# Second MLP stage of the last two token tiles: seven block products in place of eight, result feature-major, whole work order recomputed

## The chip, the cores and the metric

One NeuronCore of one Trainium2 chip runs the whole program. The metric is the device time of one execution in microseconds (us), lower is better. Engines: PE is TensorE (matmuls; PEld is its weight load), DVE is VectorE, ACT is ScalarE, POOL is GpSimd, SP issues most of the DMAs.

## What is computed

Inputs are q, k, v of shape (8 batches, 8 heads, 576 tokens, 64) and three weights, all float32. First comes linear attention with random features, then an MLP with SiLU on the 8 x 576 = 4608 tokens of width 512:

```
phi(x) = exp(h - max(h)) / sqrt(m),  h = x @ omega.T - |x|^2 / 2
num = phi(q) @ (phi(k).T @ v);  den = phi(q) @ sum(phi(k)) + 1e-6
x = num / den            # (4608, 512)
h = x @ w_in             # (4608, 2048)
g = h * sigmoid(h)
out = g @ w_out          # (4608, 512)
```

## The kernel before, in words

**Attention.** Two heads of a batch make a window; there are 32 (NWIN), four to a batch. Window n of batch t gives a quarter of the inner dimension of token tile t. The denominators of a window are ten small DVE operations (L437).

**Precision.** A float32 operand a is kept as two parts, a high one (rounded to fp32r) and a low one (the rest). A product of two such operands is three matmuls: high x high, low x high, high x low. Every MLP matmul below streams 512 columns.

**MLP, plain.** Nine token tiles of 512 tokens: tile t holds the first 512 tokens of batch t, tile 8 the last 64 of every batch. A step (t, f) belongs to token tile t and one 128-wide block f of the 2048 hidden features (16 blocks). The first stage of a step is 12 matmuls (four inner quarters x three, L633), then ACT makes SiLU twice (L743 as the rounded high part, L746 or L748 in full) and an elementwise subtraction gives the low part (L754), then the second stage is 12 matmuls (four groups of 128 tokens x three, L762) into four PSUM banks "acc". Tiles 0 to 2 (PLAIN = 3) run in this way. While tile 0 runs, the weights are loaded, converted on DVE (L595 to L601) and split on POOL (L614, L618); the parts of w_out go to DRAM (`keep_weight`) and are fetched again, 512 KB for each step (`get_weight`, L625, ring "wo" of four).

**MLP, pairs.** Tiles (3,4), (5,6) and (7,8) are taken in pairs p = 0, 1, 2. Their first stage is a two-by-two block product with seven in place of eight block multiplications (Strassen's way, in Winograd's form): the blocks are the two token tiles, two neighbouring feature blocks f = 2s and 2s + 1, and two halves of the inner dimension. For each of the eight s, `product` (L694 to L707) makes seven products of six matmuls each (L704), some added up in the same PSUM bank; ACT copies the first (`first_copy`, L711), DVE does five sums (`gather`, L730). The combined weights are prepared on POOL and ACT and kept in DRAM (`spread`, `spread_split`; L648 to L675), and come back as 28 transfers of 512 KB (`get_stream`, L692, rings x00 to x30). The combined token blocks are made at the start of a pair (`combine`, L555; `operand_high`, L562; `operand_low`, L566). The second stage of a pair is plain: 2 tiles x 16 steps x 12 matmuls. Half of it (the first tile of the pair) stands between the seven products of its s, the other half follows.

**The order.** All instructions are units of a planner (`Plan`). A unit has an engine, an estimated duration, a due time (its key), what it waits for, and the ring buffers and PSUM banks it takes. `run` goes through a model of the chip and takes at each point, among the units that could start earliest on their engine, the one with the lowest key. What it returns is the fixed instruction order of every engine, the DMA queue of SP among them. The keys come from constants (SLOW, STRETCH, PACE and others, L65 to L86) and from `shift_keys`, which moves some keys by random amounts from a list of seeds (SHIFTS). Which PSUM banks (there are eight: acc 4, att 2, h 1, fx 1) a unit may take is in `banks_of` (L97).

**The end.** The last four output banks (tile 8) are copied half by ACT (L775), half by DVE (L776), one after the other, and sent on two queues (L779).

Of the kernel before, what the change touches and what calls it, by code (L numbers as in the profile page):

```python
# [9 lines left out]
F32 = mybir.dt.float32  # L10
F32R = mybir.dt.float32r
# [8 lines left out]
P = 128  # L20
# [31 lines left out]
for _f in range(16):  # L52
# [6 lines left out]
)  # L59
EARLY_HOMES = ("wre", "wre", "hx", "s1")  # L60
STREAM = ((0, 0), (4, 1), (1, 0), (5, 1), (3, 2), (6, 1), (2, 2))
START_MLP = 54.5
SLOW = 8.26
MLP_STEP = 2.725
PRO = 11.00  # L65
SWITCH = 1.3
STAY = 7.1
# [3 lines left out]
    23, 57, 87, 139, 192, 248, 273, 481, 555, 701, 731, 750, 770, 866, 909, 936, 1096, 1151, 1552, 1831, 1917,  # L71
    1932, 2134, 2341, 2437, 2587, 2640, 270948, 271140, 273159, 273591,
# [5 lines left out]
def clock(step):  # L78
    return START_MLP + SLOW * step


STRETCH = (1.309, 1.051, 0.945)
# [3 lines left out]
PACE = ((0, clock(0)), (4, 185.0), (16, clock(NF * PLAIN) - 7.8), (24, BEGIN[1] - 8.8), (28, BEGIN[2] - 11.7))  # L86
# [22 lines left out]


def product_time(p, s, i):
    at = (0.0, 1.5, 3.3, 5.2, 8.0, 10.0, 12.5)[i]
    return BEGIN[p] + STRETCH[p] * (5.5 * MLP_STEP * s + at)


def second_time(i, j=0):
# [5 lines left out]
    if p == PAIRS:  # L122
        return BEGIN[-1]
# [15 lines left out]
class Plan:  # L139
# [16 lines left out]
    def run(self, until=None, heat=None):  # L156
# [46 lines left out]
        while any(ready.values()):  # L203
# [81 lines left out]
def attention_mlp(ctx: ExitStack, tc: tile.TileContext, qT, kT, qn, kn, v, om_in, w_in, w_out, out):  # L285
# [340 lines left out]

    def stage1(t, f, k, *ps):
# [61 lines left out]

    def get_stream(p, q):  # L690
        T["ws", p, q] = ws = new(f"x{(28 * p + q) % 4}0", [P, 2, 2, 2 * P], F32R)
        nc.sync.dma_start(ws.bitcast(F32), ws_d[q].bitcast(F32))  # L692
# [62 lines left out]

    def stage2(t, f, j):
        if f == 0 and (t or not j):
            T["po", t] = T.get(("po", t), []) + [bank("acc") for _ in range(1 if t else 4)]
        js = slice(j * P, (j + 1) * P)
        gh, gl, wo = T["gh", t, f], T["gl", t, f], T["wo", t, f]  # L760
        for n, (g, w) in enumerate(((gh, wo[:, 0]), (gh, wo[:, 1]), (gl, wo[:, 0]))):
            nc.tensor.matmul(  # L762
                T["po", t][j], g[:, js], w, start=f == 0 and n == 0, stop=f == NF - 1 and n == 2
            )

    def store(t, j):
        po = T["po", t][j]
        if t < B:
            ot = new("ot", [P, DMODEL])
            T["ot", t, j] = ot  # L770
            nc.scalar.copy(ot, po)
            return
        ot = ring.tile([P, DMODEL], F32, tag=("hk", "hq")[j % 2], name="ot", bufs=2)
        h = DMODEL // 2
        nc.scalar.copy(ot[:, :h], po[:, :h])  # L775
        nc.vector.tensor_copy(ot[:, h:], po[:, h:])  # L776
        for i in range(2):
            r = (2 * j + i) * S + MAIN
            (nc.sync, nc.scalar)[i].dma_start(out[r : r + REST], ot[i * REST : (i + 1) * REST])  # L779
# [20 lines left out]
    for n in range(NWIN):  # L800
# [95 lines left out]
        add(("den", n), "DVE", 2.9, at(n, 8, 34.2), lambda n=n: denom(n), after=e["q"] + [zn],  # L896
# [42 lines left out]
    def weight(i, key, src, last, more=()):  # L939
# [12 lines left out]
        add(("wh",) + i, "POOL", 0.64, key - 1, lambda: weight_high(i), after=[("wd",) + i + (2,)], alloc=list(more))  # L952
        add(("wlo",) + i, "POOL", 1.29, key, lambda: weight_low(i), after=[("wh",) + i], free=[("w32",) + i])

    last = None
    for f in range(NF):
        key = clock(f)
        weight(("in", f), key - 4, w_in[f], last)
# [9 lines left out]
    def products(p, s):  # L968
        for i, (c, b) in enumerate(STREAM):
            q, half = divmod(7 * s + i, 2)  # L970
            if half == 0 or i == 0 and s == 0:
# [4 lines left out]
                    after=sources, order=order, alloc=[(f"x{(28 * p + q) % 4}0", ("ws", p, q))], lat=2.1)  # L976
# [5 lines left out]
            if half or (i == 6 and s == NS - 1):  # L982
                free = free + [("ws", p, q)]
            add(m, "PE", 1.365, product_time(p, s, i), lambda *ps, p=p, s=s, i=i: product(p, s, i, *ps), after=after,
                order=order, banks=1 if i in (0, 1, 4) else 0, of="h", free=free)
            due = product_time(p, s, i) + 1.5
            if i == 0:
                add(("c1", p, s), "ACT", 0.62, due, lambda p=p, s=s: first_copy(p, s), after=[m], alloc=[("s1", ("s1", p, s))])
            else:
                for what, x in (("U2", 1), ("U3", 3), ("C22", 4), ("C21", 5), ("C12", 6)):  # L990
# [4 lines left out]
                    if what == "U2":  # L995
                        alloc = [(tags[0], ("u", p, s))] if len(tags) == 1 else [(tags[j], ("u", p, s, j)) for j in range(2)]
                    extra = {"U2": [("c1", p, s)], "C22": [("U3", p, s)], "C12": [("U2", p, s)], "C21": [("U3", p, s)]}.get(what, [("U2", p, s)])
                    free = {"C21": [bk(("m", p, s, 1))], "C12": [bk(("m", p, s, 4))]}.get(what, [])
                    add((what, p, s), "DVE", 0.69, due, lambda p=p, s=s, w=what: gather(p, s, w), after=[m] + extra, alloc=alloc, free=free)
# [3 lines left out]

    sums_of = ("odd", "S1", "even", "S2", ("split", 0), ("split", 1), "S3", ("split", 2), "even2", "S4", ("split", 3))
    for s in range(NS):
        before = ("sp", s - 1, len(sums_of) - 1) if s else ("wlo", "out", NF - 1)
        base = clock(NF + 2 + 3.3 * s)
# [33 lines left out]
    for p in range(PAIRS):  # L1041
# [8 lines left out]
        for q in range(2):  # L1050
# [19 lines left out]
            for i, (kind, what, after) in enumerate(work):  # L1070
# [9 lines left out]
                else:  # L1080
                    on = "POOL" if i % 4 == 1 else "DVE"
# [9 lines left out]
    for i, (t, f) in enumerate(steps):  # L1091
        key = clock(i)
        late = i >= total - LAG
# [32 lines left out]
        for j in range(4):  # L1126
            k2 = second_time(i, j)
            if late:
                k2 = BEGIN[-1] + 4 + 4 * j + i - total
# [8 lines left out]
            if f == NF - 1:  # L1138
                add(("store", t, j), "ACT", 0.62, k2 + 0.2, lambda t=t, j=j: store(t, j), after=[("s2", t, f, j)],
                    alloc=[("ot", ("ot", t, j))] if t < B else [], free=[("po", t, j)])  # L1140
                if t < B:
                    add(("send", t, j), "SP", 0.36, k2 + 1, lambda t=t, j=j: send(t, j), after=[("store", t, j)], lat=1.1,
                        free=[("ot", t, j)])
# [9 lines left out]
_OUT = ((B * S, DMODEL), "float32")  # L1153

# [47 lines left out]
```

## Time and profile before

| | before |
|---|---|
| median of 3 runs | 1064.47 us (1063.26 to 1065.71) |
| the profiled execution | 1064.04 us, of which span 1062.3 us |
| mean granted TensorE clock | 0.986 |
| PE busy | 96% of the span |
| DVE, ACT, POOL busy | 61%, 55%, 39% |
| first matmul of a block product (L704) | 477.5 us |
| first block product of the last pair | 885.6 us |

The span runs from the first instruction to the last; 1.7 us of the time lie around it. A busy share is an average over stages. The records of matmuls overlap (each is modelled with its latency), so 96% does not say that PE runs at its best rate; the distance between the starts of matmuls does.

### The profile page before, as it was taken

The page shows a single profiled execution, that of the slowest core. Times are in us where ns is not written, and L with a number is a line of the kernel's source. Part 1 is how long each engine was busy: PE and PEld are TensorE (multiplying, and loading weights), DVE is VectorE, ACT ScalarE, POOL GpSimd, SP SyncE. Part 2 cuts the span into 40 slices and gives each one's busy share as a digit, 9 for nine tenths or more (in the row PEclk, how much of TensorE's full clock was granted, in tenths as well). Part 3 has the DMA queues.
Part 4 walks back from the last instruction along what each step waited for, and adds up shares of the span by engine and source line. Part 5 has one row for each costly group of instructions (what it writes and reads, how often), then busy time and mean ns, then how long its engine had stood idle before and what let it go on. Part 6 is the DMA issues. An engine that isn't in the chain of part 4 may idle for free.

```text
span 1062.3 us, 16989 instructions
## 1 busy us (share of the span) xinstructions
PE 1024.3 (96%) x5926; PEld 820.4 (77%) x5926; DVE 643.9 (61%) x1665; ACT 587.1 (55%) x1033; POOL 418.7 (39%) x467
## 2 busy tenths in 40 slices
PE   6889899999999999999999999999999999999998
PEld 6667777777777777777878777788888878888886
DVE  6898798967767678777676676764535233232200
ACT  4777676656666666666545567754244464221253
POOL 2443564556565665333223245641211453000042
PEclk9788999999999999999999999999999999999999
DMA  8567565575765766557666667566554566755374
GB/s 290 186 222 234 171 213 180 194 254 181 243 222 189 240 195 210 165 180 269 205 202 196 203 204 258 176 216 215 170 174 160 193 214 207 230 187 198 116 237 139
DMA packets 82277, 216.14 MB, mean 203 GB/s; under 512 B 12944, under 2 KB 19216, under 8 KB 82192
## 3 DMA queue, kind: packets, MB, share of 16 engines
q1 hardware_dynamic: 81728, 214.47, 61.5%
q8 instruction: 47, 0.77, 0.3%
q10 hardware_dynamic: 464, 0.59, 0.2%
q14 instruction: 38, 0.31, 0.1%
HBM read 181.47 MB, written 33.55 MB: 202 GB/s over the span
## 4 chain that ended last, share of the span: by engine, by line
PE 84%; DVE 9%; issue 2%; ACT 2%; DMA 1%; POOL 1%; ACTq 0%; DVEq 0%; SPq 0%; POOLq 0%
PE ps_acc L762 33%; PE ps_h L704 11%; PE ps_fx L704 11%; PE ps_h L633 8%; PE ps_att L355 5%; DVE prod L437 4%; PE ps_att L449 3%; PE ps_att L511 2%; PE ps_att L473 2%; PE ps_fx L633 1%; PE ps_fx L473 1%; PE ps_att L362 1%; PE ps_att L420 1%; DVE nbk L376 1%; DVE mxk L371 1%
## 5 line engine op out<-in xcount | busy, mean ns | idle before, releaser
L762 PE MATMUL ps_acc<-wo,gh 128*128 128x512 f32 x1152 | 365.3, 398 | 0.0
L762 PEld LDWEIGHTS ps_acc<-wo,gh 128*128 128x128 f32 x1152 | 209.0, 188 | 43.5
L762 PE MATMUL ps_acc<-wo,gl 128*128 128x512 f32 x576 | 225.2, 391 | 0.0
L704 PE MATMUL ps_h<-w,x 128*128 128x512 f32 x504 | 130.3, 394 | 0.0
L704 PE MATMUL ps_fx<-w,x 128*128 128x512 f32 x504 | 130.1, 393 | 0.0
L633 PE MATMUL ps_h<-x,w 128*128 128x512 f32 x492 | 128.3, 402 | 0.0
L762 PEld LDWEIGHTS ps_acc<-wo,gl 128*128 128x128 f32 x576 | 108.1, 188 | 23.4
L467 POOL TENSOR_TENSOR hq<-hq,rd 128x384 f32<-128x384 f32 x96 | 83.1, 893 | 107.0 <-DVE rd L442 61.7
L704 PEld LDWEIGHTS ps_fx<-w,x 128*128 128x128 f32 x504 | 93.4, 188 | 19.9
L704 PEld LDWEIGHTS ps_h<-w,x 128*128 128x128 f32 x504 | 93.2, 188 | 20.1
L633 PEld LDWEIGHTS ps_h<-x,w 128*128 128x128 f32 x492 | 91.3, 191 | 20.2 <-ACT gf L746 0.2
L754 POOL TENSOR_TENSOR gl<-s,gh 128x512 fp32r<-128x512 f32 x24 | 31.0, 1290 | 191.0 <-ACT s L748 127.9
L754 DVE TENSOR_TENSOR gl<-gf,gh 128x512 fp32r<-128x512 f32 x72 | 57.6, 801 | 35.6 <-ACT gf L746 34.6
L437 DVE CUSTOM_DVE_ANT_0 prod<-hq,ps_att 128x128 f32<-128x128 f32 (+1 forms) x190 | 54.5, 287 | 33.0 <-ACT kw L462 13.8
L411 POOL TENSOR_TENSOR t<-hk 128x256 f32<-128x256 f32 x48 | 35.3, 757 | 98.4 <-ACT hk L405 98.4
L743 ACT ACT_TABLE_LOAD x49 | 62.9, 1283 | 1.4 <-PE ps_acc L762 0.6
L485 ACT COPY en<-ps_att 128x384 f32<-128x384 f32 x61 | 28.7, 486 | 56.9 <-PE ps_att L473 52.3
L743 ACT ACTIVATE gh<-ps_h 128x512 fp32r<-128x512 f32 x53 | 31.7, 598 | 48.2 <-PE ps_h L704 32.1
L743 ACT ACTIVATE gh<-s 128x512 fp32r<-128x512 f32 x24 | 15.2, 632 | 77.2 <-DVE s L730 70.3
L405 ACT ACT_TABLE_LOAD x40 | 51.3, 1283 | 2.0 <-DVE hk L396 1.3
L343 ACT ACTIVATE nat<-nat 128x576 f32<-128x576 f32 x64 | 42.8, 693 | 14.6 <-DMA nat<-kn 8.0
L675 POOL TENSOR_TENSOR wraw<-w,wraw 128x256 fp32r<-128x256 f32 x32 | 25.0, 782 | 53.3 <-ACT wraw L673 47.8
(245 smaller groups left out, 1820.4 us busy)
## 6 DMA issues: line engine op xcount, KB each, us to landing
wo<-wo_d SPq DMA_DIRECT2D x128, 512.0 KB, 3.9
x<-ws SPq DMA_DIRECT2D x84, 512.0 KB, 3.5
rawq<-qT SPq DMA_DIRECT2D x32, 352.0 KB, 4.0
rawk<-kT SPq DMA_DIRECT2D x32, 352.0 KB, 3.4
v<-v SPq DMA_DIRECT2D x32, 320.0 KB, 3.8
nat<-kn SPq DMA_DIRECT2D x32, 288.0 KB, 3.9
nat<-qn SPq DMA_DIRECT2D x32, 288.0 KB, 4.1
wraw<-w_in SPq DMA_DIRECT2D x16, 512.0 KB, 3.6
```

Source lines behind the costliest of these rows:

```text
L343: nc.scalar.activation(nat, nat, AF.Square, scale=SCALE * 0.5**0.5)
L355: nc.tensor.matmul(ps[:, i * M : (i + 1) * M], raw[r, o : o + P], oms[r], start=True, stop=True)
L405: nc.scalar.activation(h, h, AF.Exp)
L411: nc.gpsimd.tensor_tensor(t[:, j], e[:, 5 * j : 5 * j + 2], e[:, 5 * j + 2 : 5 * j + 4], ALU.add)
L437: nc.vector.tensor_tensor_reduce(out=prod[r], in0=e[r, c], in1=z[r, j * M : (j + 1) * M], scale=1.0, scalar=GUARD, op0=ALU.mult, op1=ALU.a ...
L467: nc.gpsimd.tensor_tensor(e[:, c], e[:, c], rd[:, c].unsqueeze(2).broadcast_to([P, 3, M]), ALU.mult)
L473: nc.tensor.transpose(ps[:, off + i * P : off + (i + 1) * P], T["h", n, "q"][:, 3 * g + i], ident)
L633: nc.tensor.matmul(ph, w[:, i], x[:, j], start=k == 0 and n == 0, stop=k == NK - 1 and n == 2)
L704: nc.tensor.matmul(ph, ws[:, u, kk * P : (kk + 1) * P], o[:, x], start=i in (0, 1, 4) and kk == 0 and n == 0, stop=kk == 1 and n == 2, ski ...
L743: nc.scalar.activation(gh, ph, AF.Silu)
L754: eng.tensor_tensor(gl, block(t, f) if held is None else held, T["gh", t, f].bitcast(F32), ALU.subtract)
L762: nc.tensor.matmul(T["po", t][j], g[:, js], w, start=f == 0 and n == 0, stop=f == NF - 1 and n == 2)
```

## The change

- The last pair's second stage becomes a block product too. Blocks: the two token tiles, two halves of 256 output features, and odd and even hidden blocks f; the eight s are added up in PSUM. Seven products i, each over s = 0 to 7, six matmuls for each (i, s) (`second`): 56 groups of six. The weight is now the stationary operand and the tokens are streamed, so that the result has features on partitions; it goes to an output of its own, `out_t`, which the host turns and puts in its place.
- The first stage of that pair now runs whole before the second (a matmul of product (0, 0) of the second stage is ordered behind the last product of the first); it may take any of the eight PSUM banks. ACT makes SiLU once in place (`whole_silu`, four for each s). DVE makes four sums for each s (`g_sum`: T3, T1, T2, T4). Then for each of the 56 groups ACT makes the high part (`g_high`) and DVE the low part (`g_rest`), in rings of three buffers.
- Combined blocks of w_out are made in the same way: the plain w_out is kept in DRAM while it is first converted (`keep_plain`, 16 transfers of 256 KB; a w32 buffer is now also held until that transfer is done), fetched later (`get_plain`, 16), combined on POOL (`spread_out`, 32 operations; `split_out`, 32 on POOL and 32 on ACT) and kept (`keep_out`, 32 transfers of 256 KB). `get_second` brings 28 x 512 KB: one transfer for products 1, 3, 4, 6, two of 256 KB for products 0, 2, 5. The 32 transfers of `get_weight` for tiles 7 and 8 are gone.
- The end: the last two result blocks are each added by DVE from PSUM (`q_out`) and sent in two parts.
- All planner constants and the list of seeds are new; some estimated durations and the model of DMA time are changed. So the order on every engine is new from the start.

The diff, cut to its core:

```diff
-START_MLP = 54.5
-SLOW = 8.26
+START_MLP = 54.500
+SLOW = 8.020
 MLP_STEP = 2.725
-PRO = 11.00
+PRO = 11.770
 SWITCH = 1.3
-STAY = 7.1
+STAY = 10.900
...
-PACE = ((0, clock(0)), (4, 185.0), (16, clock(NF * PLAIN) - 7.8), (24, BEGIN[1] - 8.8), (28, BEGIN[2] - 11.7))
+PACE = ((0, clock(0)), (4, PAIRS_4), (16, clock(NF * PLAIN) - PAIRS_16), (24, BEGIN[1] - PAIRS_24), (28, BEGIN[2] - PAIRS_28))
...
+    if u["of"] == "full":
+        return ["h", "fx", "att", "acc"]
...
-                pipe = max(pipe, t + dur + 1.0) + u["lat"]
-                done = max(pipe, t + dur + 2.2)
+                pipe = max(pipe, t + dur + 1.0) + 0.75 * u["lat"]
+                done = max(pipe + 0.25 * u["lat"], t + dur + 2.2)
...
+    def keep_plain(f):
+        nc.sync.dma_start(plain_d[f], T["w", ("out", f)])
+
+    def get_plain(s, odd):
+        T["plain", s, odd] = w = new(("gf", "w32")[odd], [P, 2, 2 * P])
+        nc.sync.dma_start(w.rearrange("p a b -> p (a b)"), plain_d[2 * s + odd])
...
+    def spread_out(s, what):
+        a11, a12, a21, a22 = plain_blocks(s)
+        if what == "S1":
+            T["S12o", s] = new("s1", [P, 2, 2 * P])
+        s1, s2 = (T["S12o", s][:, j] for j in range(2))
+        out, x, y = {"S1": (s1, a21, a22), "S2": (s2, s1, a11), "S3": (a11, a11, a21), "S4": (a12, a12, s2)}[what]
+        nc.gpsimd.tensor_tensor(out, x, y, ALU.add if what == "S1" else ALU.subtract)
+    def split_out(s, i, high):
+        if high:
+            T["spo", s, i] = new("ot", [P, 2, 2 * P], F32R)
+        g = T["spo", s, i]
+        a11, a12, _, _ = plain_blocks(s)
+        a = (T["S12o", s][:, 0], T["S12o", s][:, 1], a11, a12)[i]
+        if high:
+            nc.scalar.copy(g[:, 0], a)
+        else:
+            nc.gpsimd.tensor_tensor(g[:, 1], a, g[:, 0].bitcast(F32), ALU.subtract)
+
+    def keep_out(s, i):
+        nc.sync.dma_start(ws2_d[4 * i + s // 2][:, s % 2].bitcast(F32), T["spo", s, i].bitcast(F32))
...
+    def get_second(p, q):
+        T["wt", p, q] = ws = new(f"x{q % 4}0", [P, 2, 2, 2 * P], F32R)
+        i, s2 = divmod(q, NS // 2)
+        if i in (1, 3, 4, 6):
+            nc.sync.dma_start(ws.bitcast(F32), ws2_d[4 * {4: 0, 1: 1, 3: 2, 6: 3}[i] + s2].bitcast(F32))
+            return
+        odd, j = {0: (0, 0), 2: (1, 0), 5: (1, 1)}[i]
+        for x in range(2):
+            f = 4 * s2 + 2 * x + odd
+            nc.sync.dma_start(ws[:, x].bitcast(F32), wo_d[f][:, :, 2 * P * j : 2 * P * (j + 1)].bitcast(F32))
...
+    def whole_silu(p, s, i):
+        u = T["u", p, s]
+        src, dst = (
+            (T["pb", p, s, 0], T["b", p, s][0]), (T["s1", p, s], T["b", p, s][1]), (u[0], u[0]), (u[1], u[1]),
+        )[i]
+        nc.scalar.activation(dst, src, AF.Silu)
...
+        out, a, b, op = {
+            "T3": (x, b22, b12, ALU.subtract), "T1": (b12, b12, b11, ALU.subtract), "T2": (b11, x, b11, ALU.add),
+            "T4": (b21, b21, b11, ALU.subtract),
+        }[what]
+        nc.vector.tensor_tensor(out, a, b, op)
...
+        return (b11, b11, b21, T.get(("t3", p, s)), b12, b21, b22)[i]
+
+    def g_high(p, i, s):
+        T["qh", p, i, s] = h = new("gh", [P, MAIN], F32R)
+        nc.scalar.copy(h, g_block(p, i, s))
+
+    def g_rest(p, i, s, eng):
+        T["ql", p, i, s] = l = new("gl", [P, MAIN], F32R)
+        eng.tensor_tensor(l, g_block(p, i, s), T["qh", p, i, s].bitcast(F32), ALU.subtract)
+
+    def second(p, i, s, *ps):
+        chain = (0, 1, 0, 1, 2, 1, 2)[i]
+        if ps:
+            T["qb", p, chain] = ps
+        w = T["wt", p, i * NS // 2 + s // 2][:, s % 2]
+        h, l = T["qh", p, i, s], T["ql", p, i, s]
+        for d in range(2):
+            for n, (u, x) in enumerate(((0, h), (0, l), (1, h))):
+                nc.tensor.matmul(
+                    T["qb", p, chain][d], w[:, u, d * P : (d + 1) * P], x, start=i in (0, 1, 4) and s == 0 and n == 0,
+                    stop=s == NS - 1 and n == 2, skip_group_check=True,
+                )
...
+        ps = T["qb", p, {"C11": 0, "C21": 1, "C22": 2, "C12": 2}[what]][d]
+        T["ot", p, what, d] = ot = new("ot", [P, MAIN])
+        if what == "C11":
+            nc.scalar.copy(ot, ps)
+        else:
+            other = {"C21": T.get(("q1", p, d)), "C22": T.get(("U3", p, d)), "C12": T.get(("U2", p, d))}[what]
+            nc.vector.tensor_tensor(ot, ps, other, ALU.add)
...
-            add(("sums", n), "POOL", 3.3, at(n, 6, 25), lambda n=n: sums(n), after=e["k"], order=[("sums", n - 1)] if n > DIRECT else [],
+            add(("sums", n), "POOL", 3.4, at(n, 6, 25), lambda n=n: sums(n), after=e["k"], order=[("sums", n - 1)] if n > DIRECT else [],
...
-        add(("den", n), "DVE", 2.9, at(n, 8, 34.2), lambda n=n: denom(n), after=e["q"] + [zn],
+        add(("den", n), "DVE", 3.5, at(n, 8, 34.2), lambda n=n: denom(n), after=e["q"] + [zn],
...
+        if i[0] == "out":
+            add(("k32", i[1]), "SP", 0.36, key, lambda: keep_plain(i[1]), after=[("wd",) + i + (2,)], lat=1.1, free=[("w32",) + i])
...
-                order=order, banks=1 if i in (0, 1, 4) else 0, of="h", free=free)
+                order=order, banks=1 if i in (0, 1, 4) else 0, of="full" if full else "h", free=free)
...
+            ready = (W(0), G("T2"), W(1), G("T3"), G("T1"), G("T4"), W(3))
+            for i in range(7):
+                add(H(i), "ACT", 0.62, t1(i, s) - (4 if i else 10), lambda p=p, i=i, s=s: g_high(p, i, s), after=[ready[i]],
+                    order=[("qh", p, i, s - 1)] if s else [("qh", p, i - 1, NS - 1)] if i else [],
+                    alloc=[("gh", ("qh", p, i, s))])
+                on = "DVE"
+                add(L(i), on, 1.3 if on == "POOL" else 0.66, t1(i, s) - (3 if i else 9),
+                    lambda p=p, i=i, s=s, e=on: g_rest(p, i, s, nc.gpsimd if e == "POOL" else nc.vector),
+                    after=[H(i)], order=[("ql", p, i, s - 1)] if s else [("ql", p, i - 1, NS - 1)] if i else [],
+                    alloc=[("gl", ("ql", p, i, s))], port=True)
...
+                after = [("gt", p, q), ("qh", p, i, s), ("ql", p, i, s)]
+                if s == 0:
+                    after += {
+                        2: [("q1", p, d) for d in range(2)], 3: [("qU2", p, d) for d in range(2)],
+                        5: [("qU3", p, d) for d in range(2)], 6: [("qC22", p, d) for d in range(2)],
+                    }.get(i, [])
+                add(("m2", p, i, s), "PE", 1.365, t1(i, s), lambda *ps, p=p, i=i, s=s: second(p, i, s, *ps), after=after,
+                    order=[("m2", p, i, s - 1)] if s else [("m2", p, i - 1, NS - 1)] if i else [("m", p, NS - 1, 6)],
+                    banks=2 if i in (0, 1, 4) and s == 0 else 0, of="full",
+                    free=[("qh", p, i, s), ("ql", p, i, s)] + ([("wt", p, q)] if half else []))
...
+    out_steps = ("S1", "S2", ("split", 0), ("split", 1), "S3", ("split", 2), "S4", ("split", 3))
+    for s in range(NS):
+        base = BEGIN[PAIRS - 1] + SPREAD_AT + SPREAD_OUT * s
...
-                    on = "POOL" if i % 4 == 1 else "DVE"
+                    on = "POOL" if i % 4 == 1 and p < PAIRS - 1 else "DVE"
...
-    steps = [(t, f) for t in range(B + 1) for f in range(NF)]
+    steps = [(t, f) for t in range(PLAIN + 2 * PAIRS - 2) for f in range(NF)]
...
+    for s in range(NS):
+        products(PAIRS - 1, s)
+    second_stage(PAIRS - 1)
```

## Rows read from the trace of the kernel before

**Rows 1.** The page: busy time, and the clock in 40 slices.
```profile
PE 1024.3 (96%) x5926; PEld 820.4 (77%) x5926; DVE 643.9 (61%) x1665; ACT 587.1 (55%) x1033; POOL 418.7 (39%) x467
...
PEclk9788999999999999999999999999999999999999
```

**Rows 2.** Busy us (count) of PE, PEld, DVE, ACT, POOL, then clock, DMA, GB/s.
```profile
0.00:120.00 120.00, 100.76 (x715) 80.10 (x715) 97.26 (x273) 73.78 (x196) 47.95 (x57) 0.87 0.67 222
120.00:480.00 360.00, 347.24 (x2187) 272.87 (x2189) 272.63 (x732) 234.72 (x400) 193.45 (x235) 1.00 0.63 206
480.00:880.00 400.00, 399.17 (x2248) 321.03 (x2247) 234.51 (x605) 223.24 (x344) 140.63 (x147) 1.00 0.62 203
880.00:1057.00 177.00, 177.00 (x782) 146.38 (x780) 39.05 (x57) 55.01 (x93) 36.70 (x29) 1.00 0.57 187
```

**Rows 3.** The chain of waits, 1000 to 1063 us: start, us, what.
```profile
1005.44 47.61 PE ps_acc L762 x210
...
1057.37 0.38 ACT ot L775
...
1057.77 0.42 DVE ot L776
```

**Rows 4.** Groups by shape, 890 to 1057 us: count, busy us, mean ns.
```profile
L762 PE MATMUL ps_acc<-wo,gh 128*128 128x512 f32 x272 | 83.7, 389 | 0.0
...
L704 PE MATMUL ps_fx<-w,x 128*128 128x512 f32 x168 | 42.6, 389 | 0.0
...
L754 DVE TENSOR_TENSOR gl<-gf,gh 128x512 fp32r<-128x512 f32 x8 | 5.5, 692 | 17.8 <-ACT gf L746 17.8
...
L748 ACT ACTIVATE s<-s 128x512 f32<-128x512 f32 x8 | 5.1, 632 | 0.3
...
L730 DVE TENSOR_TENSOR w<-ps_fx,w 128x512 f32<-128x512 f32 x4 | 2.8, 692 | 7.4 <-PE ps_fx L704 7.4
...
L711 ACT COPY s<-ps_fx 128x512 f32<-128x512 f32 x4 | 2.4, 588 | 6.3 <-PE ps_fx L704 3.4 <-POOL gl L754 2.9
```

**Rows 5.** Timeline of PE: last attention product, then the last pair.
```profile
871.43 1.19 PE L511 MATMUL ps_att<-en,kw 128*64 128x512 f32 x8
...
885.60 0.62 PE L704 MATMUL ps_h<-w,x 128*128 128x512 f32 x2
```

**Rows 6.** Timeline at the end: last matmul, last DMA issue.
```profile
1056.73 0.39 PE L762 MATMUL ps_acc<-wo,gl 128*128 128x512 f32 x1
...
1058.23 0.50 ACTq L779 DMA_DIRECT2D out<-ot  x1
```

**Rows 7.** Single lines: count, ns min/median/max, first and last start.
```profile
L754 DVE TENSOR_TENSOR gl<-gf,gh x72: 630/692/1777, 87.3 to 998.5; 128x512 fp32r<-128x512 f32 x72
...
L675 POOL TENSOR_TENSOR wraw<-w,wraw x32: 727/739/1252, 228.4 to 419.8; 128x256 fp32r<-128x256 f32 x32
...
L673 ACT CAST wraw<-w x32: 387/408/429, 225.9 to 419.3; 128x256 fp32r<-128x256 f32 x32
...
L618 POOL TENSOR_TENSOR wo<-w,wo x16: 1270/1284/1400, 30.8 to 211.4; 128x512 fp32r<-128x512 f32 x16
...
L614 POOL CAST wo<-w x16: 611/648/1077, 30.0 to 210.4; 128x512 fp32r<-128x512 f32 x16
```

**Rows 8.** DMA issues: queue, count, KB each, median us to landing.
```profile
x<-ws SPq DMA_DIRECT2D x84, 512.0 KB, 3.5
...
ws<-wraw SPq DMA_DIRECT2D x32, 256.0 KB, 3.2
ws<-w SPq DMA_DIRECT2D x24, 256.0 KB, 4.6
```

**Rows 9.** Waits of the SP queue: us in total, times, longest.
```profile
SPq L574 <- DVE w L601: 64.2, 21, 6.6
```

**Rows 10.** Lines of the denominators: count, ns min/median/max.
```profile
L437 DVE DVE_READ_ACCUMULATOR2_ANT den<- x320: 73/81/84, 19.0 to 838.5; 128x1 f32 x128, 64x1 f32 x32
L437 DVE CUSTOM_DVE_ANT_0 prod<-hq,ps_att x190: 278/286/293, 140.9 to 838.3; 128x128 f32<-128x128 f32 x152, 64x128 f32<-64x128 f32 x38
```

More of the change, by code (lines that the diff above doesn't have):

```diff
@@ L284, in attention_mlp @@
 @with_exitstack
-def attention_mlp(ctx: ExitStack, tc: tile.TileContext, qT, kT, qn, kn, v, om_in, w_in, w_out, out):
+def attention_mlp(ctx: ExitStack, tc: tile.TileContext, qT, kT, qn, kn, v, om_in, w_in, w_out, out, out_t):
     nc = tc.nc
@@ L766, in store @@
     def store(t, j):
[L767 to L779, printed above, removed]
+        T["ot", t, j] = ot = new("ot", [P, DMODEL])
+        nc.scalar.copy(ot, T["po", t][j])
     def send(t, j):
@@ L957, in attention_mlp @@
         key = clock(f)
-        weight(("in", f), key - 4, w_in[f], last)
+        weight(("in", f), key - LEAD_W, w_in[f], last)
         last = ("in", f)
@@ L996, in products @@
                         alloc = [(tags[0], ("u", p, s))] if len(tags) == 1 else [(tags[j], ("u", p, s, j)) for j in range(2)]
+                        if full:
+                            alloc = room_of(p, s, "u")
                     extra = {"U2": [("c1", p, s)], "C22": [("U3", p, s)], "C12": [("U2", p, s)], "C21": [("U3", p, s)]}.get(what, [("U2", p, s)])
                     free = {"C21": [bk(("m", p, s, 1))], "C12": [bk(("m", p, s, 4))]}.get(what, [])
-                    add((what, p, s), "DVE", 0.69, due, lambda p=p, s=s, w=what: gather(p, s, w), after=[m] + extra, alloc=alloc, free=free)
+                    add((what, p, s), "DVE", 0.69, due, lambda p=p, s=s, w=what: gather(p, s, w), after=[m] + extra, alloc=alloc, free=free,
+                        order=[("num", NWIN - 1)] if full and what == "U2" and s > 1 else [])
+        if full:
+            for i, made in enumerate((("m", p, s, 2), ("C21", p, s), ("C12", p, s), ("C22", p, s))):
+                add(("ws", p, s, i), "ACT", 0.62, product_time(p, s, (2, 5, 6, 4)[i]) + 2.5, lambda p=p, s=s, i=i: whole_silu(p, s, i),
+                    after=[made] + ([("c1", p, s)] if i == 0 else []), table="silu", free=[bk(("m", p, s, 0))] if i == 0 else [])
+            return
         for j in range(2):
@@ L1031, in attention_mlp @@
                 after=[("wlo", "in", 2 * s + (i == 5)), before], lat=1.1, free=[("w", 2 * s + (i == 5))])
+    out_steps = ("S1", "S2", ("split", 0), ("split", 1), "S3", ("split", 2), "S4", ("split", 3))
+    for s in range(NS):
+        base = BEGIN[PAIRS - 1] + SPREAD_AT + SPREAD_OUT * s
+        before = [("spo", s - 1, len(out_steps) - 1)] if s else []
+        for odd in range(2):
+            add(("g32", s, odd), "SP", 0.36, base - 4, lambda s=s, odd=odd: get_plain(s, odd), lat=1.1,
+                after=[("k32", 2 * s + odd), ("gl", PLAIN + 2 * PAIRS - 4, NF - 2)], order=[("g32", s, 0)] if odd else [("g32", s - 1, 1)] if s else [],
+                alloc=[(("gf", "w32")[odd], ("g32", s, odd))])
+        before = before + [("g32", s, odd) for odd in range(2)]
+        for i, what in enumerate(out_steps):
+            split = isinstance(what, tuple)
+            alloc = [("s1", ("s12", s))] if what == "S1" else []
+            after = before
+            if split:
+                add(("spoh", s, i), "ACT", 0.4, base + i - 0.8, lambda s=s, i=what[1]: split_out(s, i, True), after=after,
+                    alloc=[("ot", ("spot", s, what[1]))])
+                after = [("spoh", s, i)]
+            f = (lambda s=s, i=what[1]: split_out(s, i, False)) if split else (lambda s=s, w=what: spread_out(s, w))
+            frees = [("s12", s)] + [("g32", s, odd) for odd in range(2)] if i == len(out_steps) - 1 else []
+            add(("spo", s, i), "POOL", 0.75, base + i, f, after=after, alloc=alloc, free=frees,
+                order=[("cb", PAIRS - 1, q, "T4") for q in range(2)] if s == 0 and i == 0 else [])
+            before = [("spo", s, i)]
+            if split:
+                add(("spok", s, what[1]), "SP", 0.36, base + i + 2, lambda s=s, i=what[1]: keep_out(s, i), after=before, lat=1.1,
+                    free=[("spot", s, what[1])])
     for k in range(NK):
@@ L1092, in attention_mlp @@
         key = clock(i)
-        late = i >= total - LAG
+        late = False
         if t:
@@ L1139, in attention_mlp @@
                 add(("store", t, j), "ACT", 0.62, k2 + 0.2, lambda t=t, j=j: store(t, j), after=[("s2", t, f, j)],
[L1140 to L1143, printed above, removed]
+                    alloc=[("ot", ("ot", t, j))], free=[("po", t, j)])
+                add(("send", t, j), "SP", 0.36, k2 + 1, lambda t=t, j=j: send(t, j), after=[("store", t, j)], lat=1.1,
+                    free=[("ot", t, j)])
+    for s in range(NS):
+        products(PAIRS - 1, s)
+    second_stage(PAIRS - 1)
     shift_keys(plan.units.values())
@@ L1197 @@
     o = nc.dram_tensor("out", _OUT[0], F32, kind="ExternalOutput").ap()
+    ot = nc.dram_tensor("out_t", _OUT_T[0], F32, kind="ExternalOutput").ap()
     with tile.TileContext(nc) as tc:
-        attention_mlp(tc, *args, o)
+        attention_mlp(tc, *args, o, ot)
     r = run_bass_kernel_spmd(nc, [arrays], core_ids=[0])
-    return r.results[0]["out"]
+    whole, turned = r.results[0]["out"], r.results[0]["out_t"]
+    got = whole.reshape(B, S, DMODEL).copy()
+    tiles = turned.T.reshape(2, MAIN, DMODEL)
+    got[B - 1, :MAIN] = tiles[0]
+    got[:, MAIN:] = tiles[1].reshape(B, REST, DMODEL)
+    return got.reshape(B * S, DMODEL)
```

142 lines of the change are left out of this document (128 added, 14 removed).

## The prediction

> **What bounds the kernel now.** I read the page first, for who is busy: PE, 96% of the span, next DVE with 61%; the granted clock is below 1.0 only in the first slices [rows 1]. A busy share does not say whether PE streams at its best rate, so next come the windows, one for each kind of stage [rows 2]. In the first 120 us PE is idle for 120 - 100.8 = 19.2 us at a mean clock of 0.87; in the rest of the plain tiles, to 480 us, for 12.8 us; to 880 us for 0.8 us; from 880 to 1057 us not at all, at a clock of 1.00, which is the 2.4 GHz level. Then the chain of waits for the end: 210 second-stage matmuls follow each other for 47.61 us [rows 3], which is 0.2267 us each. The records show 0.389 us a matmul [rows 4], because they overlap; the distance is the price, not the record. Last, the timeline of PE: the last attention product starts at 871.4 us, the last pair's first block product at 885.6 us [rows 5]. From there to the last matmul (start 1056.73 us, [rows 6]) there is no attention left and nothing holds PE back. The last pair has 336 + 384 = 720 matmuls, 720 x 0.2267 = 163.2 us; the other 21 of the 184.5 us from 872.6 to 1057.1 us go to leftovers of pair 1. So in this stage a matmul taken away is time taken away, if what feeds PE keeps pace.
>
> **Term 1, matmuls removed.** The second stage of tiles 7 and 8 has 2 tiles x 16 steps x 12 = 384 matmuls, the new one 7 products x 8 s x 6 = 336. Both stream 512 columns. 48 x 0.2267 = **-10.9 us**, all on the path.
>
> **Term 2, the first stage of the last pair alone.** Before, second-stage matmuls stood between its seven products; now they follow directly. A product lasts 6 x 0.2267 = 1.36 us. Product 2 needs ACT's copy of product 0, with product 1 between: from the end of a matmul to the start of ACT's copy 0.25 us (1056.73 + 0.39 to 1057.37, [rows 3, 6]), the copy 0.59 [rows 4], about 0.03 to the next: 0.87 of 1.36 us. Products 3, 5 and 6 need a DVE sum, 0.25 + 0.69 [rows 4] + 0.05 = 0.99 of 1.36 us. What is queued ahead can spoil it: a SiLU of 0.63 [rows 4] begun just before adds at most 0.63 - 0.49 = 0.14 us, a DVE sum 0.69 - 0.37 = 0.32 us. For each s there are one and three such places: 8 x (0.14 + 3 x 0.32) = 8.8 us is the upper end, 0 the lower. A gain is excluded, since PE did not idle here before. ACT has 0.59 + 4 x 0.63 = 3.1 us and DVE 7 x 0.69 = 4.8 us of work in the 9.5 us of an s, so most arrive at a free engine: I take +1.0.
>
> **Term 3, feeding the second stage.** For each of 56 groups of 1.36 us ACT makes a high part (0.63) and DVE a low part (0.69) [rows 4]. In total ACT has 56 x 0.63 + 4 x 0.59 = 37.6 us, DVE 56 x 0.69 + 16 sums (T2, T4) x 0.69 + 10 result sums x 0.69 = 56.6 us, in 76.2 us: both fit. The tight spot is the ring of three: the buffer of group n comes free when group n - 3 ends, two groups (2.72 us) before it is wanted; 0.25 + 0.63 + 0.03 + 0.69 + 0.05 = 1.65 us is needed. One sum in front on DVE still fits, 2.34. With a sum in each of eight groups running DVE has 1.38 us of work in 1.36 us. The product changes wait for a copy or sum that has a whole product of 8 x 1.36 us to be done in. Lower end 0; the upper end is the rival below. I take +0.5.
>
> **Term 4, preparing w_out.** Added on POOL are 64 operations of about 0.74 us (47 us), on ACT 32 of 0.41 us (13 us) [rows 7], at a pace of one s in 10 us around the start of the last pair. POOL has room there: 140.6 us busy in the 400 us before 880, and 36.7 of 177 us after, most of which falls away with the low parts that it made there [rows 2]. On SP's queue 64 transfers of 256 KB and 40 issues for the second stage come in, 32 of 512 KB go: some 15 MB more beside a DMA share near 0.6 [rows 2]. The streams of the last pair still ask for 512 KB in 2.72 us, as before, from rings refilled 8.2 us ahead; they land in 3.5 us, pieces of 256 KB in 3.2 to 4.6 us [rows 8]. Cover is the ring's lead; I take 0, and put its loss under the rivals.
>
> **Term 5, the end.** Before, 1.11 us lie between the last matmul's end and the last DMA issue (1057.12 to 1058.23, [rows 6]): two copies in turn. Now the last block's sum starts as the earlier one, whose matmuls end 0.68 us sooner, is done: 0.25 + 0.69 + 0.04 = 0.98. -0.1.
>
> **Term 6, the new order before 880 us.** No row prices an order. What it can win or lose is bounded by PE's idle time there, 19.2 + 12.8 + 0.8 = 32.8 us [rows 2]; most of it is waiting for the first data and chains inside the attention, which no order removes, so I bound both sides by a quarter, 8 us. The estimated duration of the denominators goes from 2.9 to 3.5 us; ten operations of 0.287 + 0.081 [rows 10] make 3.7, so the planner's model comes nearer to the chip, and DVE fills more of the first 480 us than it thought. I take -1.0.
>
> **Sum.** 1064.0 (the profiled execution, 1062.3 in the span and 1.7 around it) - 10.9 + 1.0 + 0.5 + 0 - 0.1 - 1.0 = **1053.5 us**. That execution stands 0.4 us under the median shown, which is nothing here: a measurement of this kernel tells apart about 0.2%, 2.1 us.
>
> **Rivals.** *DVE holds PE in the last pair.* For it: a low part on DVE takes from 0.63 up to 1.78 us over the whole run [rows 7], and 0.69 in the last pair, where POOL is mostly quiet [rows 4]. If POOL's preparation of w_out runs late, into product 0, each low part there is over budget by 1.78 - 1.36 = 0.42 us, 3.4 us for eight, and the eight T2 behind them add 5.5 us; with the 8.8 us of term 2 cut to a few the loss is 5 to 11 us. Against it: POOL is due to be done some 35 us before. Time 1058 to 1064, chance 0.12. The Trainium skill, page "GPSIMD Engine Reference", section "1. Specifications", says that GpSimd shares its SBUF interfaces with VectorE and contends with instructions that have two SBUF inputs. By that rule this rival holds wherever both work; the 1.78 us agree with it, and the forecast lives from POOL being quiet.
>
> *The first tile is held by the keeping of w_out* (the other side). For each of 16 blocks SP gets a transfer that waits for DVE's conversion, ahead of loads of weights and attention inputs; and the w32 buffer stays taken until it lands. SP already waits for that DVE line 21 times, 64.2 us in all [rows 9], 3.1 us each. The buffer was free after POOL's 0.65 + 1.28 = 1.9 us [rows 7]; a 256 KB transfer needs its issue and 3.2 to 4.6 us [rows 8]. Here PE idles and nothing covers a delay [rows 2]. Price: 16 x up to 3.1 = 50 us; it turns the sign when more than 13 / 16 = 0.8 us of each lands on the path. Against it: 32 weights pass in some 190 us [rows 7], so three buffers leave 18 us for each, and about 8 are needed. 1067 to 1078, chance 0.10.
>
> *The new order gives more*: a quarter of the idle time comes back, 1042 to 1048, chance 0.14. *The weights of the second stage are late*: products 0, 2 and 5 take two transfers each; if SP is held up behind another wait by more than the 8.2 - 4.6 = 3.6 us of lead, a few of 12 such pairs cost 1 to 3 us: 1056 to 1063, chance 0.04. That the change would not take matmuls away has no room: the count is fixed.
>
> **Numbers.** The forecast, with its own range 1048 to 1058, has 0.60. The range 1044 to 1063 holds it, most of the first rival and of the larger gain, and leaves out the slower one. Faster by over 0.2% (under 1062.3): 0.60 + 0.14 + 0.10 of the two middle rivals = 0.84; within 0.2%: 0.07; slower: 0.09.
>
> **What would show it.** Matmuls of the last pair at 0.227 us from its first product to the end, 672 of them in 152 to 155 us, none waiting for ACT or DVE for more than a few tenths. Wrong: gaps of PE every 1.36 us in the last pair (terms 2 and 3), low parts of over 1 us there (DVE rival), PE idle well over 32 us before 880 us (first tile), or a first block product of the last pair that is later than 885.6 us.

## The result, and the profile after

The changed kernel takes 1047.55 us (median of 4 runs, 1046.07 to 1049.35) against 1064.72 us: ratio 0.9841, 95% interval 0.9821 to 0.9861, 17.2 us less. The forecast was 1053.5 us, 11.2 us less. The profiled execution of after took 1046.07 us, span 1044.0 us.

The page of the changed kernel, its busy times and the clock in 40 slices:

```profile
PE 1010.4 (97%) x5878; PEld 808.4 (77%) x5878; DVE 696.2 (67%) x1757; ACT 596.4 (57%) x1073; POOL 427.5 (41%) x501
...
PEclk9888999899999999999999999999999999999999
```

There are 48 matmuls fewer than in [rows 1], 5878 for 5926. DVE has 52 us more to do, POOL 9, ACT 9. The windows of the changed kernel (columns as in [rows 2]):

```profile
0.00:120.00 120.00, 102.56 (x745) 81.78 (x746) 99.14 (x275) 80.53 (x210) 48.75 (x58) 0.90 0.71 238
120.00:480.00 360.00, 350.70 (x2230) 276.56 (x2229) 274.83 (x760) 224.50 (x386) 192.89 (x239) 0.99 0.65 217
480.00:880.00 400.00, 397.86 (x2208) 319.03 (x2207) 227.74 (x588) 218.65 (x347) 140.27 (x152) 1.00 0.62 210
880.00:1035.00 155.00, 154.98 (x683) 127.81 (x682) 92.15 (x133) 72.04 (x131) 45.54 (x55) 1.00 0.76 258
```

The last line is the new last pair: PE is idle for 0.02 us, and 683 matmuls in 155 us are one in 0.2269 us, the pace of the old one [rows 3]. So the 48 matmuls are gone and nothing has taken their place. The upper lines belong to stages whose matmuls the change leaves as they were, and yet PE is idle there for 17.4 + 9.3 + 2.1 = 28.9 us in place of 32.8 [rows 2], and between 120 and 480 us 2230 matmuls are seen in place of 2187. The timeline of PE shows where the early stages end, at the last attention product (L533) and the first block product of the last pair (L775):

```profile
849.73 1.19 PE L533 MATMUL ps_att<-en,kw 128*64 128x512 f32 x8
850.85 1.43 PE L775 MATMUL ps_h<-w,x 128*128 128x512 f32 x5
```

The attention is done 21.7 us sooner than in [rows 5]. From its last product's end (850.9) to the last matmul's (1038.93 + 0.39 = 1039.3, below) are 188.4 us; 672 matmuls of the pair take 152.3 of them, so 36 us are second stage of pair 1 that was put off (156 of its matmuls still come after the attention), where before it was 21. Of the 21.7 us some 15 are thus paid back as work still to do; nearly 7 are won. The end, in the timeline of the changed kernel:

```profile
1038.93 0.39 PE L881 MATMUL ps_fx<-gh,x 128*128 128x512 f32 x1
...
1039.35 0.69 DVE L903 TENSOR_TENSOR ot<-ps_fx,w 128x512 f32<-128x512 f32 x1
```

From the last matmul's end to the span's end are 4.7 us, before 1062.3 - 1057.1 = 5.2 [rows 6]. The span is 18.3 us shorter: 10.9 by the matmuls, 0.5 by the end, 6.9 by what lies before. (The profiled execution is the fastest of four; by the medians the last figure is about 6.)

### The profile page after: what moved, and what is told of

Its sections match the earlier page's. It is cut to its first block, busy times and chain, and to the rows that moved or that the text cites. A ratio compares the mean times of both kernels' runs of the same rounds, so it can differ in the third digit from the quotient of the medians.

```text
span 1044.0 us, 17291 instructions
## 1 busy us (share of the span) xinstructions
PE 1010.4 (97%) x5878; PEld 808.4 (77%) x5878; DVE 696.2 (67%) x1757; ACT 596.4 (57%) x1073; POOL 427.5 (41%) x501
## 4 chain that ended last, share of the span: by engine, by line
PE 79%; DVE 13%; DMA 3%; ACT 2%; issue 2%; SPq 0%; POOL 0%; DVEq 0%; ACTq 0%; POOLq 0%
PE ps_acc L920 26%; PE ps_fx L775 8%; PE ps_h L691 8%; PE ps_h L775 8%; PE ps_acc L881 4%; DVE prod L459 4%; PE ps_att L377 3%; PE ps_acc L775 3%; PE ps_att L471 2%; PE ps_att L775 2%; PE ps_att L533 2%; PE ps_fx L691 2%; PE ps_att L495 2%; PE ps_h L881 2%; DMA nat<-kn 1%
## 5 line engine op out<-in xcount | busy, mean ns | idle before, releaser
L920 PE MATMUL ps_acc<-wo,gh 128*128 128x512 f32 x896 | 286.7, 401 | 0.0
L920 PEld LDWEIGHTS ps_acc<-wo,gh 128*128 128x128 f32 x896 | 161.7, 189 | 33.7
L920 PE MATMUL ps_acc<-wo,gl 128*128 128x512 f32 x448 | 175.7, 392 | 1.2 <-POOL gl L839 1.2
L775 PE MATMUL ps_h<-w,x 128*128 128x512 f32 x396 | 102.3, 394 | 0.2 <-DVE w L815 0.2
L775 PE MATMUL ps_fx<-w,x 128*128 128x512 f32 x396 | 102.4, 394 | 0.0
L920 PEld LDWEIGHTS ps_acc<-wo,gl 128*128 128x128 f32 x448 | 84.2, 188 | 20.0 <-POOL gl L839 1.6
L775 PEld LDWEIGHTS ps_fx<-w,x 128*128 128x128 f32 x396 | 73.3, 188 | 16.5 <-DVE hq L815 0.3
L775 PEld LDWEIGHTS ps_h<-w,x 128*128 128x128 f32 x396 | 73.3, 188 | 16.4 <-DVE w L815 0.6
L881 PE MATMUL ps_acc<-gh,x 128*128 128x512 f32 x112 | 43.6, 389 | 0.0
L393 DVE TENSOR_REDUCE mxk<-ps_att 128x4 f32<-128x512 f32 x48 | 31.4, 685 | 11.8 <-PE ps_att L377 10.5
```

The costliest lines, as they stand in the source:

```text
L393: nc.vector.tensor_reduce(m[:, 5 * j : 5 * j + 4], ps.rearrange("p (c m) -> p c m", m=M), AX.X, ALU.max)
L775: nc.tensor.matmul(ph, ws[:, u, kk * P : (kk + 1) * P], o[:, x], start=i in (0, 1, 4) and kk == 0 and n == 0, stop=kk == 1 and n == 2, ski ...
L881: nc.tensor.matmul(T["qb", p, chain][d], w[:, u, d * P : (d + 1) * P], x, start=i in (0, 1, 4) and s == 0 and n == 0, stop=s == NS - 1 and ...
L920: nc.tensor.matmul(T["po", t][j], g[:, js], w, start=f == 0 and n == 0, stop=f == NF - 1 and n == 2)
```

## The experiments

Three theories stood at the start. A: matmuls on a dense PE give 10.9 us, the new order of the first 880 us the rest. B: the last pair gives more than its matmuls. C: matmuls are hidden behind another engine. All times are medians; ratios are to the kernel before, measured beside each run.

| run | edit | us | ratio, 95% interval |
|---|---|---|---|
| changed kernel | | 1047.55 | 0.9841 (0.9821 to 0.9861) |
| x1_b_48less | before, 48 matmuls out | 1053.92 | 0.9892 (0.9877 to 0.9906) |
| x2_a_48more | changed, 48 matmuls more | 1057.67 | 0.9927 (0.9909 to 0.9945) |
| x3_a_noshift | changed, no seeds | 1056.18 | 0.9907 (0.9883 to 0.9930) |
| x4_a_noplain | changed, plain w_out not kept | 1047.61 | 0.9824 (0.9808 to 0.9840) |
| x5_b_noshift | before, no seeds | 1072.14 | 1.0066 (1.0046 to 1.0086) |
| x6_b_newkeys | before, new constants and durations, no seeds | 1059.92 | 0.9953 (0.9935 to 0.9971) |
| x7_a_oldkeys | changed, old constants, no seeds | 1057.24 | 0.9926 (0.9910 to 0.9943) |
| x8_a_poollow | changed, a quarter of the low parts on POOL | 1046.60 | 0.9827 (0.9809 to 0.9846) |
| x9_a_any1 | changed, six arbitrary seeds | 1052.68 | 0.9889 (0.9876 to 0.9902) |
| x10_a_any2 | changed, six others | 1059.81 | 0.9952 (0.9938 to 0.9965) |
| x11_a_picked | changed, seeds picked by the planner's model | 1053.39 | 0.9897 (0.9878 to 0.9916) |
| x12_a_robust | changed, seeds picked under disturbance | 1046.91 | 0.9837 (0.9824 to 0.9849) |

**What 48 matmuls are worth, at an unchanged order.** In the kernel before:

```diff
         for n, (g, w) in enumerate(((gh, wo[:, 0]), (gh, wo[:, 1]), (gl, wo[:, 0]))):
+            if t >= B - 1 and n == 1 and 2 <= f < 8:
+                continue
             nc.tensor.matmul(
```

> The kernel before in its own order, with 48 matmuls fewer in the second stage of tiles 7 and 8 (the high x low pass of six steps of either tile is left out, so those tiles come out less exact). Theory A, matmuls on a dense PE: 48 x 0.2267 = 10.9 us less, 1064.7 to 1053.8, with no new wait. Theory B, a good part of the gain of the change comes from something else that leaves with the old second stage (its transfers, the SiLU made twice): the same edit brings clearly less than 10.9 us, or the new kernel gains from its last pair more than this. Theory C, matmuls are hidden behind another engine: less than 5 us.

In the changed kernel:

```diff
-            for n, (u, x) in enumerate(((0, h), (0, l), (1, h))):
+            for n, (u, x) in enumerate(((0, h), (0, l), (1, h), (0, h), (0, l), (1, h)) if i == 3 else ((0, h), (0, l), (1, h))):
...
-                    stop=s == NS - 1 and n == 2, skip_group_check=True,
+                    stop=s == NS - 1 and n == (5 if i == 3 else 2), skip_group_check=True,
```

> The changed kernel in its own order, with the six matmuls of product 3 made twice for each of the eight s (48 more, the result of those blocks is wrong by that product). Theory A: 10.9 us more, 1047.6 to 1058.5; with that the changed kernel with as many matmuls as before is still about 6 us faster than before, and these 6 us belong to the order of the first 880 us. Theory B: the time rises by less than 10.9 us, because the second stage waits on DVE and the extra matmuls fill the waits.

Measured: 11.3 us less than the 1065.23 us of before beside it, and 10.1 us more than the changed kernel. By the intervals of the ratios the first is 10.0 to 13.1 us. For the second two ratios have to be taken from each other, 0.9927 and 0.9841, which gives 9.2 us, give or take some 3. Both hold 10.9, and both last pairs are dense. The window from 880 to 1035 us of the kernel with 48 more (columns as in [rows 2]):

```profile
880.00:1035.00 155.00, 154.99 (x684) 127.89 (x683) 85.17 (x124) 67.28 (x123) 43.91 (x54) 1.00 0.72 242
```

And that from 880 to 1040 us of the one with 48 fewer:

```profile
880.00:1040.00 160.00, 160.00 (x708) 132.56 (x707) 38.45 (x54) 53.57 (x90) 36.47 (x28) 1.00 0.65 207
```

In the last pair of either kernel a matmul costs PE the same, within what can be measured. Theories B and C fall. What is left of the 17.2 us, about 6, is not in the last pair: with as many matmuls as before, the changed kernel (1057.67 us) is still 7.6 us faster than the 1065.23 of before.

**The seeds of the order.** The list SHIFTS is made empty, in the changed kernel (whose diff is shown) and in the one before:

```diff
-SHIFTS = (
...
-)
+SHIFTS = ()
```

> The changed kernel with an empty list of seeds, so no key is moved at random; all else is the same. If the 6 us beyond the matmuls come from the keys and estimated durations, the time stays within 2 us of 1047.6; if they come from the random moves, it rises by some 4 to 7 us, to 1052 to 1055. The last pair should stay as dense either way.

> The kernel before with an empty list of seeds. The random moves were worth 8.6 us in the changed kernel (1056.2 without against 1047.6 with). If they are worth about as much in the kernel before, this one takes some 1070 to 1074 us, and then the seeds alone do not explain why the new order is better than the old; if they are worth little there (1065 to 1068), the 6 us beyond the matmuls are the better list of seeds.

Without its list the changed kernel loses 8.6 us, the kernel before 6.6 (1065.58 beside it). Against an empty list both are worth about as much to their kernels, so by this comparison the new one is not simply the better list. The changed kernel without seeds, in windows:

```profile
0.00:120.00 120.00, 99.81 (x724) 79.73 (x725) 100.60 (x272) 79.62 (x206) 48.87 (x57) 0.91 0.71 232
120.00:480.00 360.00, 344.77 (x2165) 271.38 (x2164) 268.45 (x724) 219.62 (x380) 190.05 (x235) 0.98 0.66 209
...
880.00:1035.00 155.00, 154.91 (x683) 127.64 (x682) 84.75 (x123) 73.69 (x135) 53.68 (x66) 1.00 0.79 269
```

The loss is in the first 480 us: PE idle for 20.2 + 15.2 = 35.4 us in place of 26.7, with 2165 matmuls between 120 and 480 us in place of 2230. The last pair is as dense as ever.

**The constants of the keys.** In the kernel before, the new SLOW, PRO, STAY, STRETCH, PACE and offsets together with the new durations and DMA model; in the changed kernel, the old constants with the new durations; both without seeds (lines of the first are shown):

```diff
-SLOW = 8.26
+SLOW = 8.02
...
-        add(("den", n), "DVE", 2.9, at(n, 8, 34.2), lambda n=n: denom(n), after=e["q"] + [zn],
+        add(("den", n), "DVE", 3.5, at(n, 8, 34.2), lambda n=n: denom(n), after=e["q"] + [zn],
...
```

> The kernel before (plain second stage of all pairs) with the changed kernel's constants for the keys, its estimated durations and its model of DMA time, and no seeds; the partner of the changed kernel without seeds (1056.2 us), so between these two stand the matmuls alone. Theory A: 1056.2 + 10.9 - 0.6 = 1066.5 us. And if the new keys and durations are the better ones, it is faster than the kernel before without seeds; if they are worth nothing, the same within 2 us.

> The changed kernel with the old constants for the keys of the first 880 us (SLOW, PRO, STAY, the stretches and paces), the new estimated durations, no seeds. If the new constants carry the better order, it is slower than the changed kernel without seeds (1056.2): 1060 to 1066. If the constants do not matter once the seeds are out, 1054 to 1058.

The first missed: 1059.9, not 1066.5, only 3.7 us above its partner. The second says that the constants do not matter: 1057.2, one microsecond over its partner. In the kernel before, constants and durations together were worth 12.2 us (x5 to x6), in the changed one the constants alone 1.1. These do not add up to a price for any constant. No run changes the durations and the DMA model alone, so what they are worth is not shown. Each edit of a key or of the set of units gives another order from the first microsecond on, and orders scatter; the next runs show by how much.

**How far orders scatter.** The changed kernel with six arbitrary seeds (x9: 753159, 367853, 877820, 475951, 823985, 875839; x10: 783704, 655787, 130414, 588240, 361150, 780499):

> The changed kernel with six arbitrary seeds in place of its list: random moves of keys that nobody chose. If the list of the change is one good order picked out of many that scatter, arbitrary moves give no gain over no moves (1056.2 us) and may lose: 1053 to 1066. If any loosening of the keys helps, the time comes near 1047.6. The last pair stays dense in both.

> As the run before with six other arbitrary seeds, for the scatter: 1053 to 1066 if the list of the change was a picked one; the planner's own model puts this order later than the one before it, so if that model is any guide on the chip, this one is the slower of the two by several us.

They are 7.1 us apart, in the order in which the planner's model had put them; one is better than no seeds, one worse. With x3 and x7 there are four orders of the changed kernel whose seeds no search had picked: 1052.7, 1056.2, 1057.2 and 1059.8 us, mean 1056.5. PE's idle time in the first 880 us goes with them: 28.9 us in the changed kernel, 35.8 in x9, 36.4 in x3, 36.0 in x7 and 42.1 in x10, the slowest, whose line is (columns as in [rows 2])

```profile
0.00:880.00 880.00, 837.93 (x5098) 667.11 (x5099) 613.71 (x1619) 521.63 (x932) 367.12 (x431) 0.98 0.65 211
```

The list of the change is 9 us better than the mean of the four. The kernel before has two such orders, x5 and x6: 1072.1 and 1059.9 us, mean 1066.0, and its own list is 1.3 us better than that. From mean to mean the step is 9.5 us, near the matmuls alone, so the extra gain may well be a better pick out of the scatter. That is not shown, since two orders 12 us apart make a poor mean. Taken in pairs, x5 to x3 and x5 to x7, the changed kernel is 16.0 and 14.9 us ahead without any list, which is 5.1 and 4.0 more than its matmuls.

**Can the search go on?** Two longer lists, grown from the list of the change, a move kept if the planner's model ends earlier (46 seeds) or if the mean of six disturbed executions does (74 seeds):

> The changed kernel with a longer list of seeds, each new one kept only if the planner's own model ended earlier with it. If the model is a guide on the chip, the order gains again, 1043 to 1046; if the list of the change is already as far as the model can tell, or I fit the model's errors, 1046 to 1052.

> The changed kernel with a list of seeds picked in the same way, but judged by the mean over six executions of the fixed order with durations, hand-overs and transfers disturbed at random. If orders fail on the chip because they fit exact durations, this list does better than the list picked by the exact model: 1041 to 1045. If not, the same as that one within 2 us.

The list picked by the exact model lost 5.8 us on the chip, as a list would that fits the model's errors; no run tells that from the scatter of orders. The one picked under disturbance is the changed kernel's equal (0.9837 to 0.9841), not better. No version here beats the changed kernel by more than can be measured.

**The keeping of w_out in the first tile.** The 16 transfers are left out; the later fetch reads the high part from the split weights (and waits for those, a line not shown):

```diff
     def keep_plain(f):
-        nc.sync.dma_start(plain_d[f], T["w", ("out", f)])
+        pass
...
-        nc.sync.dma_start(w.rearrange("p a b -> p (a b)"), plain_d[2 * s + odd])
+        nc.sync.dma_start(w.rearrange("p a b -> p (a b)"), wo_d[2 * s + odd][:, 0].bitcast(F32))
...
```

> The changed kernel without the 16 transfers that keep the plain w_out in the first tile; the later fetch reads the high part of w_out in their place, which lacks the low bits in the combined blocks. Order unchanged. The rival of the prediction (the keeping holds the first tile) expects a gain of several us, up to 1040 to 1044; my forecast had it hidden: within 1.5 us of 1047.6.

1047.61 against 1047.55 us: nothing that can be measured, with the instructions of PE, DVE, ACT and POOL in the same order. The slower rival of the prediction had a place but no force.

**Room on DVE in the second stage.** Low parts of s = 1 and s = 5 go to POOL:

```diff
-                on = "DVE"
+                on = "POOL" if s % 4 == 1 else "DVE"
```

> The changed kernel with every fourth pair of low parts of the second stage (s = 1 and s = 5) on POOL in place of DVE. A low part takes POOL 1.29 us, so the chain for such a group takes 2.25 us of the 2.72 us that a ring of three gives, and beside it DVE's two-input operations may take up to 1.78 us. The rival of the prediction (DVE and the shared access hold PE in the last pair, little room) expects PE to wait there: 3 to 8 us more, 1051 to 1056. If the feeding has the room that I worked out, it stays within 2 us of 1047.6.

1046.6 us, no loss. The single lines of the low parts in this run (ns min/median/max):

```profile
L871 DVE TENSOR_TENSOR gl<-w,gh x4: 691/709/1055, 914.2 to 1018.4; 128x512 fp32r<-128x512 f32 x4
L871 POOL TENSOR_TENSOR gl<-en,gh x4: 1282/1319/1586, 968.2 to 1022.6; 128x512 fp32r<-128x512 f32 x4
```

A low part on POOL takes up to 1.59 us, so its chain takes 0.25 + 0.63 + 0.03 + 1.59 + 0.05 = 2.55 us of the ring's 2.72, and PE stays at 154.97 of 155 us busy.

## Why the prediction was right, and where its size was off

The time lies in the range, on the side that was forecast. It lies just outside the likeliest case's own range (1048 to 1058) and inside that of the rival "new order gives more" (1042 to 1048). No errors cancelled: every term that was off came out on the faster side.

- **Term 1** (-10.9 us) is right and shown from both sides: -11.3 with 48 matmuls fewer, +10.1 with 48 more, orders unchanged.
- **Terms 2 and 3** (+1.5 us) were too cautious. The products of the first stage stand between second-stage matmuls of pair 1 until 904 us, follow each other directly until 963 us, and then the second stage runs (columns as in [rows 2]):

```profile
904.00:963.00 59.00, 58.98 (x260) 48.28 (x259) 33.12 (x46) 24.70 (x50) 27.20 (x34) 1.00 0.89 308
963.00:1039.00 76.00, 76.00 (x337) 62.87 (x335) 51.62 (x78) 35.84 (x59) 0.00 (x0) 1.00 0.60 197
```

By the starts of its 258 matmuls (58.5 us at 0.2267 each) the first of these stretches loses about 0.5 us, the second nothing. The chains of 0.87, 0.99 and 1.65 us against 1.36 and 2.72 us are met even with a quarter of the low parts on the slower engine. The upper ends (8.8 us; the DVE rival, 5 to 11 us) never came near. The condition of the DVE rival did not come either: POOL's last work on w_out ends at 945.9 us, 17 us before the second stage starts (35 were forecast), and POOL does nothing after (0.00 above). The Trainium skill, page "GPSIMD Engine Reference", section "1. Specifications", has GpSimd and VectorE share their SBUF interfaces, with contention for VectorE instructions of two SBUF inputs. The 1.06 us of a low part of x8, at 914.2 us beside a busy POOL, agree with it; that it would hold PE here, the 1046.6 us deny.
- **Term 4** (0) is right in the sum, though the traffic is less harmless than "15 MB more" made it. It comes in one piece. The changed kernel in windows (DMA share and GB/s last):

```profile
900.00:920.00 20.00, 20.00 (x90) 16.57 (x89) 13.47 (x18) 10.11 (x23) 13.03 (x15) 1.00 0.99 351
920.00:940.00 20.00, 19.98 (x88) 16.03 (x87) 10.61 (x15) 8.77 (x20) 13.59 (x17) 1.00 1.02 355
```

For 40 us the DMA engines have no room left, and PE stays busy all the same. The order picked under disturbance (x12) loses 1.25 us of PE in the same 40 us, 1.12 of them in one wait:

```profile
916.96 0.41 ACT L682 CAST ot<-gf 128x256 fp32r<-128x256 f32 x1 [3.13 <-DMA wt<-ot]
...
920.27 0.56 ACT L800 COPY hq<-ps_acc 128x512 f32<-128x512 f32 x1
...
920.89 1.43 PE L779 MATMUL ps_acc<-w,x 128*128 128x512 f32 x5 [1.12 <-ACT hq L800]
```

ACT, which works in a fixed order, waits 3.13 us for a buffer that a transfer of the w_out preparation still holds. Its work then stands in line until the copy of product 0, for which PE waits: the wait of term 2, "what is queued ahead", set off by the traffic. This is read from the trace; no run tests it.
- **Term 5** (-0.1) measured -0.5, counted to the span's end. The last sum begins as the matmul ends (1039.32 to 1039.35), not 0.25 us after; the hand-over had been taken from ACT.
- **Term 6** (-1.0) is the one mis-sized: about -6. The bound of 8 us on either side held, the value inside it did not. I argued that most idle time was waiting no order removes and so put the gain near zero. Idle time fell from 32.8 to 28.9 us, 3.9 of the 6.9 us in the profiled executions. The other 3 lie in stretches where PE counts as busy, which a bound from idle time leaves out; they were not taken apart. So the rival "new order gives more" (0.14) had the right time, but by half of the idle time that it asked for. Four unpicked orders of the same work spread over 7 us, and the searched one lies 5 us below the best of them. What in the new constants, durations and seeds makes this order good stays open: x3, x5, x6 and x7 redraw the whole order, and their differences do not agree as prices.
- **The slower rival** (keeping w_out, 0.10) is refuted by x4. **The late weights** (0.04) did not come: pieces of 256 KB for products 0, 2, 5 landed in 3.1 us (median), the 512 KB of the others in 4.0. What did get slower are the 512 KB streams of this pair's first stage, 5.1 us where the last pair of before had 3.3; both are within the 8.2 us of the rings' lead.

## What to carry to other kernels

Where the timeline shows PE dense with no other bound near, a removed matmul is worth the distance between matmul starts; 48 x 0.227 us came out within 0.8 us by the medians, in the last pair of either kernel. Where an order is computed by a planner and then searched, price a change of structure at a fixed order (take matmuls out of the old, put them into the new), because an edit of the plan redraws the order and can move the time by several microseconds for reasons of its own. A search on a model may do better to judge candidates under disturbed durations: the exact model's order was 6 us worse on the chip than the other's. That is one pair of lists, within the scatter of 7 us, so it is a hint and not shown.

## What the runs showed of the hardware that I had not expected

PE's half clock shows in the middle of the changed kernel. At 188 us PE waits 4.2 us for DVE, once (us, times, longest):

```profile
PE ps_att L471 <- DVE hq L421: 4.2, 1, 4.2
```

The windows from there on (PE's busy time first, then PEld, DVE, ACT, POOL, granted clock):

```profile
188.00:193.00 5.00, 0.82 (x6) 0.42 (x7) 4.76 (x9) 3.43 (x5) 1.88 (x2) 0.87 0.57 225
193.00:196.00 3.00, 3.00 (x24) 2.31 (x22) 2.86 (x5) 0.00 (x0) 0.46 (x1) 0.50 0.40 89
196.00:200.00 4.00, 4.00 (x16) 2.84 (x13) 0.83 (x2) 1.45 (x4) 3.84 (x5) 0.68 0.64 218
200.00:204.00 4.00, 4.00 (x20) 3.27 (x20) 2.96 (x8) 1.44 (x2) 1.07 (x3) 1.00 0.31 105
```

After the wait PE is busy but at the 1.2 GHz level (0.50) for three microseconds and partly for four more: (1 - 0.50) x 3 + (1 - 0.68) x 4 = 2.8 us of full-rate work lost on top of the 4.2. By this estimate even the better order holds a place worth up to 7 us; no run here tried to mend it.
